# Attention outputs of the last two blocks computed in pairs of tiles on the upper and lower rows of the PE array

## The chip, the cores and the metric

The kernel runs on one core of a Trainium2 chip. The metric is the device time of one execution in microseconds (us); the median of several runs is compared. The core's engines are named as in the profile: PE (TensorE, matrix products; PEld are its weight loads), DVE (VectorE), ACT (ScalarE), POOL (GpSimd) and SP (SyncE, which issues DMAs here).

## The reference

Two kinds of layer alternate, four layers in all, on 2048 tokens of 576 features in bfloat16. Layers 0 and 2 are linear attention with 32 heads of 18 features, layers 1 and 3 an MLP with 4608 hidden units:

```python
x = x + attention(layernorm(x), wqkv, wo)
x = x + mlp(layernorm(x), w1, b1, w2, b2)
x = x + attention(layernorm(x), wqkv, wo)
x = x + mlp(layernorm(x), w1, b1, w2, b2)

# attention, per head
pq, pk = phi(q), phi(k)                  # phi(t) = t + 1 for t > 0, exp(t) otherwise, plus 1e-6
kv, z = pk.T @ v, pk.sum(over tokens)
o = (pq @ kv) / (pq @ z + 1e-6)
out = concat(o over heads) @ wo

# mlp (its input is normalised once more)
h = gelu(layernorm(y) @ w1 + b1)
out = h @ w2 + b2
```

## The kernel before

The tokens are cut into 16 tiles of 128 rows and four blocks of four tiles (c = 0 to 3 in the code; the title's blocks 3 and 4 are c = 2 and 3). A matmul takes a stationary operand, loaded by a weight load of its own, and streams the moving one; the sum over the contracted rows builds up in a bank of PSUM. Everything on PE goes through `mm` (L223, shown as L224 in the profile), which writes PE's order down by hand, in the order of the calls; an `InOrder` wrapper (L45, shown as L53) does the same for DVE, ACT, POOL and SP. So the order of each engine's work is the order of the code.

**Attention outputs.** The 32 heads form five groups, four of seven heads (126 features) and one of four (72, of which 64 rows stand in its own array and the other eight in the spare rows 126 and 127 of the first four groups). `pq[(g, c)]` holds group g of block c, features by tokens; two blocks share one array for group 4, even blocks in rows 0 to 63, odd ones in rows 64 to 127. `kvwo[g]` is the product of kv and wo, 576 columns; for group 4 there are two copies, one with content in the upper 64 rows and zeros below, and `wo_odd` the other way round (L644 to L648). `wo_stage(t)` (L701) makes a tile's output: for each of two halves of 288 columns five matmuls over 128 rows, one for each group, into one bank of a pair of banks; `residual` (L461) then adds both halves to `x_sb` with one DVE instruction.

Ahead of the outputs of a block stands `scales(c)`: DVE multiplies its five `pq` arrays by the reciprocal denominators, which SP's DMAs have spread over the rows (`spread`, L677).

**MLP groups.** `m1_group` (L822) makes four hidden tiles (f = 4g to 4g + 3) for 512 tokens. Here the contraction of 576 is cut at 64 rows: nine products of 64 rows for each tile, 36 in all, issued by turns to the upper and lower 64 rows of the array, which work side by side. Upper rows take the tiles in the order 0, 1, 2, 3, lower rows in the order 2, 3, 0, 1. Two halves of the array never write the same bank at once: before a half goes on with a tile that the other half began, it waits for a relay, a tiny ACT copy (`relay_sb`), which itself waits for the other half's last matmul on that bank (L847 to L867). After that ACT evicts the four tiles through the gelu.

Nine such groups belong to the MLP's first block. Eight of them are already issued within the attention layer, between the output stages, so that PE has work while the denominators go round:

```python
scales(1)
groups(3)
den_stage(2)
den_stage(3)
spread(2)
spread(3)
outputs(1)
scales(2)
scales(3)
groups(3)
outputs(2)
outputs(3)
groups(2)
```

PSUM: `pair` (L73) hands out two double banks by turns, `one` (L85) four single banks by turns. A group takes a pair and two singles, a `wo_stage` a pair.

Of the kernel before, what the change touches and what calls it, by code (L numbers as in the profile page):

```python
# [8 lines left out]
ALU = mybir.AluOpType  # L9
BF16 = mybir.dt.bfloat16  # L10
F32 = mybir.dt.float32
PSUM = bass.MemoryType.PSUM
# [3 lines left out]
P = 128  # L16
# [11 lines left out]
TPC = CB // P  # L28
CA = 512
NCA = S // CA  # L30
HALF = D // 2
# [4 lines left out]
def build(tc, A_x, A_wqkv, A_wo, B_w1, B_b1, B_w2, B_b2, out, n_layers=4):  # L36
    nc = tc.nc
    with ExitStack() as ctx:
        const = ctx.enter_context(tc.tile_pool(name="const", bufs=1))
# [21 lines left out]
        SYNC = mybir.DependencyInfo(mybir.DependencyClass.Sync, mybir.DependencyReason.DATA)  # L61
        vec, act = InOrder(nc.vector, "VectorE"), InOrder(nc.scalar, "ScalarE")
        pool, sp = InOrder(nc.gpsimd, "GpSimd"), InOrder(nc.sync, "SyncE")
# [9 lines left out]
        def pair(name, tag=None):  # L73
            if tag is None:
                pair_turn["n"] += 1
                tag = ("accA", "accB")[pair_turn["n"] % 2]
            return ps_pair.tile([P, 2, 512], F32, name=name, tag=tag)
# [3 lines left out]
        def one_tag():  # L81
            one_turn["n"] += 1
            return f"one{one_turn['n'] % one_turn['banks']}"

        def one(name, tag=None):  # L85
            return ps_one.tile([P, 512], F32, name=name, tag=tag or one_tag())
# [105 lines left out]
        x_sb = const.tile([P, NT, D], BF16, name="x_sb")  # L192
# [12 lines left out]
        wo_odd = const.tile([P, D], BF16, name="wo_odd")  # L205
        kvwo_rows = dpool.tile([8, D], BF16, name="kvwo_rows")
        relay_sb = const.tile([P, 2], F32, name="relay_sb")
        sums_sb = const.tile([P, 4], F32, name="sums_sb")
        y_rows = [dpool.tile([CB, D], BF16, name=f"y_rows{c}") for c in range(NCB)]
        rden_rows = [dpool.tile([H, CA], BF16, name=f"rden_rows{c}") for c in range(NCA)]  # L210
# [6 lines left out]
        def pe(inst):  # L217
            if pe_last["last"] is not None:
                tc.add_manual_dep(inst.ins, pe_last["last"], NOSYNC, reason="TensorE order")
            pe_last["last"] = inst.ins.name  # L220
            return inst

        def mm(out_, lhsT, rhs, start, stop, **kw):  # L223
            return pe(nc.tensor.matmul(out_, lhsT=lhsT, rhs=rhs, start=start, stop=stop, **kw))  # L224


        def load_x(t, by=sp):
# [189 lines left out]
        def by_token(ap, placed):  # L417

            return ap.rearrange("p (t b q) -> p b t q", t=4, b=4) if placed else ap

        def as_read(ap, placed):
            return ap.rearrange("p (b t q) -> p b t q", b=4, t=4) if placed else ap
# [24 lines left out]
        def two(ap):  # L447
            return ap.rearrange("p (h n) -> p h n", h=2)
# [12 lines left out]
        def residual(li, t, halves):  # L461
            xo = xo_of.pop(t)[:] if t in xo_of else x_sb[:, t, :]
            vec.tensor_tensor(out=two(x_sb[:, t, :]), in0=halves, in1=two(xo), op=ALU.add)
            if li == n_layers - 1:
                sp.dma_start(out=out_f[t * P:(t + 1) * P, :], in_=x_sb[:, t, :])

        def layer_A(li, next_kind, begin, before_tile, before_keys, mid_tile, rows_ahead, after_tile, q_tiles, placed, mlp):
            es, pks, kps, vas, pq, ys = {}, {}, {}, {}, {}, {}
            acc = {}
# [23 lines left out]
            def k_finish(t):  # L493
                k_sum(t, 0)
                return k_sum(t, 1)
# [74 lines left out]
            for t in range(NT):  # L570
                before_tile(t)
                if placed:
# [10 lines left out]
                    done = k_finish(t)  # L583
                    if TPC <= t < TPC + NT - NX:
                        ys[t - TPC + NX] = placed_rows(t - TPC + NX)
                else:
# [14 lines left out]
                    if t == 1:  # L601
                        done = k_sum(2, 1)
                    mid_tile(t)
                    rows_ahead(t)
                    if 1 < t < NT - 1:
                        done = k_finish(t + 1)
# [23 lines left out]
            kvwo = {}  # L630
# [70 lines left out]
            def wo_stage(t):  # L701
                c, j = divmod(t, TPC)
                wp = pair("wo_ps")
                for half in range(2):
                    for g in range(G):
# [2 lines left out]
                           by[:, half * HALF:(half + 1) * HALF], g == 0, g == G - 1)  # L708
                residual(li, t, wp[:, :, 0:HALF])


            first = [Norm(t, "B", "act" if t < 3 else "dve", "act" if t == 0 else "dve") for t in range(TPC)]

# [3 lines left out]
                              in1=side[0:126, 0:260].rearrange("p (g c) -> p g c", g=4)[:, :, 64:65].to_broadcast([126, 4, H]),  # L717
                              op=ALU.mult)
            vec.tensor_copy(out=products[0:65, 4, 0:V4].rearrange("p (g d) -> p g d", g=4), in_=tp[0:65, :, 0:126])
            vec.tensor_copy(out=zk[96:P, :].rearrange("p (i c) -> p i c", i=2),  # L720
                            in_=side[96:P, 264:328].unsqueeze(1).to_broadcast([32, 2, 64]))
# [3 lines left out]
                                     in1=sums_sb[96:P, :], op0=ALU.mult, op1=ALU.add)  # L725
            vec.tensor_tensor(
                out=kvT[0:72, 4, 0:72].rearrange("p (h e) -> p h e", h=4),
                in0=side[0:72, 264:336].rearrange("p (h e) -> p h e", h=4),
                in1=maskz[0:72, 0:4, :], op=ALU.mult)
# [3 lines left out]
            for k in range(KD):  # L733
                rows = slice(0, P if k < 4 else 65)
                for g in range(4):
# [5 lines left out]
                              in1=zp[:, 0:1].unsqueeze(1).to_broadcast([P, 2, H]), op=ALU.mult)  # L741
            vec.tensor_tensor(
                out=kvT[0:126, 0:4, :].rearrange("p g (h e) -> p g h e", h=7),
                in0=kvp[0:126, 0:V4].rearrange("p (g h e) -> p g h e", g=4, h=7),
                in1=maskz[0:126, :, :].unsqueeze(1).to_broadcast([126, 4, 7, DH]), op=ALU.mult)
# [40 lines left out]
            def scales(c):  # L786
                for g in range(G):
                    scale_stage(g, c)

            def groups(n):  # L790
                for _ in range(n):
                    mlp.m1_group(0, mlp.done)
                    mlp.flush()

            def outputs(c):
                for t in range(c * TPC, (c + 1) * TPC):
                    wo_stage(t)
# [8 lines left out]
            outputs(1)  # L806
            scales(2)
            scales(3)
            groups(3)
            outputs(2)  # L810
            outputs(3)
            groups(2)

        GF = 4
        NGRP = NF // GF

        class LayerB:
# [4 lines left out]
            def m1_group(self, c, g):  # L822
                hT = self.hT.setdefault(c, {})
                ctok = slice(c * CB, (c + 1) * CB)

                early = [one("h_ps") for _ in range(2)]
                late = pair("hp_ps")
                dst = [late[:, 0, :], early[0][:], late[:, 1, :], early[1][:]]

                def half_blocks(n, hi):  # L830
                    f = g * GF + n
                    rows = slice(64 * hi, 64 * hi + 64)
                    ops = [(n, w1_sb[rows, k, f * P:(f + 1) * P], yT[rows, k, ctok]) for k in range(KD - 1)]
                    if f % 2 == hi:
                        fc = f // 2 * P
                        ops.append((n, w1_tail[rows, fc:fc + P], yT[rows, KD - 1, ctok]))
                    return ops

                upper = [op for n in (0, 1, 2, 3) for op in half_blocks(n, 0)]
                lower = [op for n in (2, 3, 0, 1) for op in half_blocks(n, 1)]  # L840
                seen = [0] * GF
                order = [(hi, n, wt, mv) for step in zip(upper, lower) for hi, (n, wt, mv) in enumerate(step)]
                first, final = {}, {}
                for i, (hi, n, _, _) in enumerate(order):
                    first.setdefault((hi, n), i)
                    final[(hi, n)] = i
                relay_at = {final[(0, 0)]: (0, 2), final[(1, 3)]: (1, 3)}  # L847
                starts = {first[(1, 0)]: 0, first[(0, 2)]: 2, first[(1, 1)]: 1, first[(0, 3)]: 3}
                relay_of = {}

                def evict(n):
                    f = g * GF + n
                    hT[f] = units[:, f, :]
                    out_ = act.activation(out=by_token(hT[f], c > 0), in_=as_read(dst[n], c > 0),
                                          func=ACT.Gelu_apprx_tanh, bias=b1T[:, f:f + 1], scale=1.0)
                    gate["after"] = out_.ins.name

                for i, (hi, n, wt, mv) in enumerate(order):
                    ins = mm(dst[n], wt, mv, seen[n] == 0, seen[n] == 8)
                    seen[n] += 1  # L860
                    if i in starts:
                        tc.add_manual_dep(ins.ins, relay_of[starts[i]], SYNC, reason="row tiles take turns on a PSUM bank")
                    if i in relay_at:
                        relay = act.copy(out=relay_sb[:, 1:2], in_=relay_sb[:, 0:1])
                        tc.add_manual_dep(relay.ins, ins.ins.name, SYNC, reason="row tiles take turns on a PSUM bank")
                        for m in relay_at[i]:
                            relay_of[m] = relay.ins.name  # L867
                        if i == final[(0, 0)]:
                            self.flush()
                    if n in (0, 2) and seen[0] == seen[2] == 9:  # L870
                        evict(0)
                        evict(2)
                    if n == 1 and seen[1] == 9:
                        evict(1)
                self.held = lambda: evict(3)
                self.done += 1

# [209 lines left out]
```

## Time and profile before

| | |
|---|---|
| median of 3 runs | 751.42 us (751.21 to 751.78) |
| the profiled execution | 751.55 us, span 749.8 us |
| PE busy | 745.2 us, 99% of the span |
| DVE, ACT, POOL busy | 269.1, 298.4, 114.9 us |
| outputs of blocks 3 and 4, first attention layer | from 110.7 us of the span on |
| the same, second attention layer | from 478.3 us on |

The span runs from the first to the last instruction of the program. In a timeline's row the columns are start, duration, engine, line, operation, written tile <- read tiles, shape, count, and in brackets the engine's idle time before it and what ended it; consecutive instructions of one kind are merged, and their durations overlap, since matmuls are pipelined. A row of the stages gives for a window its length, then busy time and number of instructions for PE, PEld, DVE, ACT and POOL, the granted clock of PE, and the DMA share and rate. `hp_ps` and `h_ps` are the banks of an MLP group, `wo_ps` those of the outputs, `m_ps` those of the MLP's second product.

### The profile page before, as it was taken

How to read it: one execution, taken by the hardware profiler on the slowest of the kernel's cores; microseconds unless marked ns; L12 is line 12 of the kernel's file. 1: busy time of each engine (PE TensorE's matmuls, PEld its weight loads, DVE VectorE, ACT ScalarE, POOL GpSimd, SP SyncE). 2: the span in 40 equal slices, each digit the busy share in tenths (PEclk: the TensorE clock that was granted, in tenths of full speed). 3: DMA queues.
4: the chain of work that ended last, by engine and by line, in shares of the span. 5: the costliest groups of instructions: out<-in, count | busy, mean ns of one | idle time of the engine just before them, and what ended most of it. 6: DMA issues, size and time to landing. Idle time of an engine off the chain costs nothing.

```text
span 749.8 us, 15361 instructions
## 1 busy us (share of the span) xinstructions
PE 745.2 (99%) x6437; PEld 468.6 (63%) x6437; DVE 269.1 (36%) x654; ACT 298.4 (40%) x652; POOL 114.9 (15%) x245
## 2 busy tenths in 40 slices
PE   9999999999999999999999999999999999999998
PEld 5666455774576457646766665657646754774476
DVE  8987644334124303401365586432400140100000
ACT  5657743106601740374045474440274047205700
POOL 4541100322011201201200020022200120010010
PEclk9999999999999999999999999999999999999999
DMA  7991120022011202110032001102000200020000
GB/s 200 250 354 52 35 68 2 11 49 45 1 27 41 38 1 44 35 26 1 24 109 63 2 9 59 44 1 51 19 1 1 59 10 1 14 46 10 1 12 21
DMA packets 60381, 34.48 MB, mean 46 GB/s; under 512 B 36728, under 2 KB 60312, under 8 KB 60312
## 3 DMA queue, kind: packets, MB, share of 16 engines
q1 hardware_dynamic: 59560, 33.27, 17.4%
q8 instruction: 50, 0.82, 0.4%
q10 hardware_dynamic: 752, 0.23, 0.1%
q14 instruction: 19, 0.16, 0.1%
HBM read 21.70 MB, written 4.93 MB: 36 GB/s over the span
## 4 chain that ended last, share of the span: by engine, by line
PE 99%; DVE 0%; DMA 0%; issue 0%
PE m_ps L224 38%; PE hp_ps L224 21%; PE h_ps L224 17%; PE k_ps L224 6%; PE wo_ps L224 5%; PE q_ps L224 5%; PE rk_ps L224 4%; PE tp L383 1%; PE side_ps L224 1%; PE den_ps L224 0%; PE kvwo_ps L224 0%; PE kv_ps L224 0%; DMA x_sb<-in_A_x_dram 0%; PE rden_ps L224 0%; DVE ln_st L53 0%; PE side_tp L629 0%
## 5 line engine op out<-in xcount | busy, mean ns | idle before, releaser
L224 PEld LDWEIGHTS <-units 128*128 128x128 bf16 x2688 | 260.2, 98 | 74.5 <-issue 4.6
L224 PE MATMUL m_ps<-w_sb,units 128*128 128x288 bf16 (+2 forms) x2304 | 283.6, 286 | 0.0
L224 PEld LDWEIGHTS <-w_sb 64*128 64x128 bf16 x2304 | 123.9, 94 | 136.8 <-ACT relay_sb L53 4.1
L224 PE MATMUL h_ps<-yT,w_sb 64*128 64x512 bf16 x1152 | 178.0, 376 | 0.0
L224 PE MATMUL hp_ps<-yT,w_sb 64*128 64x512 bf16 x1152 | 148.0, 376 | 0.1
L53 DVE TENSOR_TENSOR x_sb<-m_ps,xo 128x576 bf16<-128x576 f32 (+2 forms) x33 | 24.4, 739 | 324.6 <-PE m_ps L224 324.6
L53 ACT COPY relay_sb<-relay_sb 128x1 f32<-128x1 f32 x144 | 27.7, 192 | 264.2 <-PE hp_ps L224 246.6
L53 ACT ACTIVATE units<-hp_ps,b1T 128x512 bf16<-128x512 f32 x144 | 91.2, 684 | 59.3 <-PE hp_ps L224 58.5
L53 POOL TENSOR_TENSOR xo<-x_sb,b_bc 128x576 f32<-128x576 bf16 x32 | 40.8, 1275 | 407.5 <-DVE x_sb L53 298.6
L53 ACT ACTIVATE units<-h_ps,b1T 128x512 bf16<-128x512 f32 x144 | 96.2, 688 | 0.0
L224 PE MATMUL hp_ps<-yT,w_tail 64*128 64x512 bf16 x144 | 54.1, 376 | 0.0
L224 PE MATMUL h_ps<-yT,w_tail 64*128 64x512 bf16 x144 | 54.1, 376 | 0.0
L224 PE MATMUL k_ps<-wkv_sb,yT 128*128 128x288 bf16 (+1 forms) x320 | 52.8, 302 | 0.0
L53 DVE BATCH_NORM_STATS2 ln_st<-x_sb 128x6 f32<-128x288 bf16 x128 | 51.3, 440 | 1.2 <-DMA x_sb<-in_A_x_dram 0.9
L53 ACT ACTIVATE phi_e<-k_ps 128x288 bf16<-128x288 f32 x64 | 26.4, 414 | 52.1 <-PE k_ps L224 50.7
L53 DVE STREAM_TRANSPOSE shared<-y_ring 128x640 bf16<-128x640 bf16 x40 | 32.9, 826 | 39.6 <-DMA yT<-shared 38.0
L53 ACT ACTIVATE units<-q_ps 128x512 bf16<-128x512 f32 x72 | 38.4, 596 | 21.4 <-PE q_ps L224 21.2
L53 DVE TENSOR_SCALAR y_ring<-x_sb,ln_mv,ln_rstd 128x576 bf16<-128x576 bf16 (+2 forms) x58 | 31.1, 538 | 40.7 <-POOL ln_rstd L53 40.5
L224 PE MATMUL q_ps<-yT,wq_sb 128*128 128x512 bf16 (+1 forms) x200 | 44.5, 380 | 0.0
L224 PE MATMUL wo_ps<-shared,units 128*128 128x288 bf16 x288 | 40.7, 286 | 0.0
L224 PEld LDWEIGHTS <-w_tail 64*128 64x128 bf16 x288 | 27.1, 94 | 17.0
L53 POOL TENSOR_TENSOR ln_rstd<-ln_u,neg_half 128x1 f32<-128x1 f32 x64 | 36.1, 564 | 8.5 <-DVE ln_u L53 3.5
(96 smaller groups left out, 421.1 us busy)
## 6 DMA issues: line engine op xcount, KB each, us to landing
yT<-shared SPq DMA_DIRECT2D x160, 40.0 KB
w_sb<-in_B_w_dram SPq DMA_DIRECT2D x12, 432.0 KB
w_sb<-in_B_w_dram SPq DMA_DIRECT2D x9, 512.0 KB
yT<-rden_rows SPq DMA_DIRECT2D x24, 126.0 KB
y_rows<-y_ring SPq DMA_DIRECT2D x16, 144.0 KB
units<-y_rows SPq DMA_DIRECT2D x16, 144.0 KB
x_sb<-in_A_x_dram SPq DMA_DIRECT2D x15, 144.0 KB
out_dram<-x_sb SPq DMA_DIRECT2D x15, 144.0 KB
```

The costliest lines, as they stand in the source:

```text
L53: inst = issue(*args, **kw)
L224: return pe(nc.tensor.matmul(out_, lhsT=lhsT, rhs=rhs, start=start, stop=stop, **kw))
L383: pe(nc.tensor.transpose(out=tp[:, k - a, :], in_=self.y[:, k * P:(k + 1) * P], identity=ident[:]))
```

## The change

The loop that issues 64-row matmuls by turns with its two relays is taken out of `m1_group` into a function, `row_tiles`; the MLP groups call it with ACT's copy as relay and keep their order. A new `wo_pair(t, u)` uses the same function for the outputs of two tiles, t of block 3 and u = t + 4 of block 4. The four accumulators are t's two halves (in a pair of banks) and u's two halves (in two single banks). Each group's product is cut at row 64; group 4 is issued for its 64 rows with content alone. The relay is a memset on POOL of one value per row (`pool_relay`). DVE adds t's halves with one instruction and u's with two. The order of the stages becomes `groups(4)`, four pairs, `groups(1)`, in place of `groups(3)`, eight single tiles, `groups(2)`.

```diff
+        pool_relay = const.tile([P, 1], F32, name="pool_relay")
...
+        def row_tiles(ops_of, dst, relay, after):
+            order = [(hi, op) for step in zip([op for n in (0, 1, 2, 3) for op in ops_of(n, 0)],
+                                              [op for n in (2, 3, 0, 1) for op in ops_of(n, 1)]) for hi, op in enumerate(step)]
+            first, final, total = {}, {}, [0] * 4
+            for i, (hi, (n, _, _)) in enumerate(order):
+                first.setdefault((hi, n), i)
+                final[(hi, n)] = i
+                total[n] += 1
+            relay_at = {max(final[(0, a)], final[(1, b)]): (a, b) for a, b in ((0, 2), (1, 3))}
+            starts = {first[(1, 0)]: 0, first[(0, 2)]: 2, first[(1, 1)]: 1, first[(0, 3)]: 3}
+            relay_of, seen = {}, [0] * 4
+            for i, (hi, (n, wt, mv)) in enumerate(order):
+                ins = mm(dst[n], wt, mv, seen[n] == 0, seen[n] == total[n] - 1)
+                seen[n] += 1
+                if i in starts:
+                    tc.add_manual_dep(ins.ins, relay_of[starts[i]], SYNC, reason="row tiles take turns on a PSUM bank")
+                if i in relay_at:
+                    passed = relay()
+                    tc.add_manual_dep(passed.ins, ins.ins.name, SYNC, reason="row tiles take turns on a PSUM bank")
+                    for m in relay_at[i]:
+                        relay_of[m] = passed.ins.name
+                after(n, [a == b for a, b in zip(seen, total)], relay_at.get(i))
...
+            def wo_pair(t, u):
+                late, early = pair("wo_ps"), [one("wo_ps") for _ in range(2)]
+
+                def ops_of(n, hi):
+                    (c, j), rows = divmod((t, u)[n // 2], TPC), slice(64 * hi, 64 * hi + 64)
+                    tok, cols = slice(j * P, (j + 1) * P), slice(n % 2 * HALF, (n % 2 + 1) * HALF)
+                    ops = [(n, pq[(g, c)][rows, tok], kvwo[g][rows, cols]) for g in range(4)]
+                    if c % 2 == hi:
+                        ops.append((n, pq[(4, c)][rows, tok], kvwo[4][hi][rows, cols]))
+                    return ops
+
+                row_tiles(ops_of, [late[:, 0, 0:HALF], late[:, 1, 0:HALF]] + [acc[:, 0:HALF] for acc in early],
+                          lambda: pool.memset(pool_relay[:], 0.0), lambda *a: None)
+                residual(li, t, late[:, :, 0:HALF])
+                for half, acc in enumerate(early):
+                    rows = x_sb[:, u, half * HALF:(half + 1) * HALF]
+                    vec.tensor_tensor(out=rows, in0=acc[:, 0:HALF], in1=rows, op=ALU.add)
...
-            groups(3)
-            outputs(2)
-            outputs(3)
-            groups(2)
+            groups(4)
+            for t in range(2 * TPC, 3 * TPC):
+                wo_pair(t, t + TPC)
+            groups(1)
...
-                for i, (hi, n, wt, mv) in enumerate(order):
-                    ins = mm(dst[n], wt, mv, seen[n] == 0, seen[n] == 8)
...
+                row_tiles(half_blocks, dst, lambda: act.copy(out=relay_sb[:, 1:2], in_=relay_sb[:, 0:1]), after)
```

More of the change, by code (lines that the diff above doesn't have):

```diff
@@ L837, in half_blocks @@
                     return ops
[L839 to L849, printed above, removed]
                 def evict(n):
@@ L856, in evict, with after @@
                     gate["after"] = out_.ins.name
-                for i, (hi, n, wt, mv) in enumerate(order):
-                    ins = mm(dst[n], wt, mv, seen[n] == 0, seen[n] == 8)
[L860 to L870, printed above, removed]
+                def after(n, done, turn):
+                    if turn == (0, 2):
+                        self.flush()
+                    if n in (0, 2) and done[0] and done[2]:
                         evict(0)
                         evict(2)
-                    if n == 1 and seen[1] == 9:
+                    if n == 1 and done[1]:
                         evict(1)
+                row_tiles(half_blocks, dst, lambda: act.copy(out=relay_sb[:, 1:2], in_=relay_sb[:, 0:1]), after)
                 self.held = lambda: evict(3)
```

## The prediction

> **What bounds the kernel now.** I read the page's header and chain first, then the timeline of PE around the outputs, then the stages. The page:
>
> ```profile
> span 749.8 us, 15361 instructions
> ...
> PE 745.2 (99%) x6437; PEld 468.6 (63%) x6437; DVE 269.1 (36%) x654; ACT 298.4 (40%) x652; POOL 114.9 (15%) x245
> ...
> PE 99%; DVE 0%; DMA 0%; issue 0%
> ```
>
> TensorE (PE) is busy for 745.2 of 749.8 us, and the chain that ends last is 99% PE. So whatever PE time an edit takes away or adds comes out at the end, unless a wait replaces it. The profiled execution took 751.55 us, 1.75 more than its span, and 0.13 above the median of 751.42.
>
> The timeline of PE around block 3 and 4's outputs in the first attention layer:
>
> ```profile
> 110.41 0.38 PE L224 MATMUL h_ps<-yT,w_tail 64*128 64x512 bf16 x1
> 110.72 5.56 PE L224 MATMUL wo_ps<-shared,units 128*128 128x288 bf16 x44
> 116.12 0.29 PE L224 MATMUL wo_ps<-wo_odd,units 128*128 128x288 bf16 x1
> ...
> 120.41 0.29 PE L224 MATMUL wo_ps<-wo_odd,units 128*128 128x288 bf16 x1
> 120.62 1.04 PE L224 MATMUL hp_ps<-yT,w_sb 64*128 64x512 bf16 x8
> ```
>
> Between the two wo_odd rows lie 35 matmuls (seven half tiles of five): 4.29 us, 0.1226 us each. The recorded 0.29 us overlaps the following ones, so the pitch of starts is the cost. An MLP group for comparison, and five matmuls of 512 columns on the full array:
>
> ```profile
> 102.85:106.74 3.89, 3.89 (x40) 1.71 (x37) 1.76 (x5) 2.70 (x8) 0.00 (x0) 1.00 0.32 104
> ```
> ```profile
> 43.53 1.24 PE L224 MATMUL q_ps<-yT,wq_sb 128*128 128x512 bf16 x5
> ```
>
> One group runs from one hp_ps row at 102.85 to that of the next at 106.74: 18 steps, in each of which the upper and the lower 64 rows work at once, 0.216 us a step. Five full-array matmuls of the same width give (1.24 - 0.38)/4 = 0.215. Two 64-row matmuls side by side thus take the time of one full one, and the group keeps that pace through its two relays.
>
> **The change part by part.**
>
> *Removed.* The last 64-row step before the outputs starts at 110.41 and lasts 0.216, so the outputs occupy PE from 110.62 to 120.62. The windows of both layers:
>
> ```profile
> 110.62:120.62 10.00, 10.00 (x82) 7.75 (x81) 5.73 (x8) 1.76 (x4) 0.00 (x0) 1.00 0.01 2
> ...
> 478.18:488.18 10.00, 10.00 (x82) 7.75 (x81) 5.30 (x7) 1.76 (x4) 0.00 (x0) 1.00 0.01 2
> ```
>
> 10.00 us per layer. Of these 80 x 0.1226 = 9.81 are matmuls; the other 0.19 are two gaps of about 0.095, where PE goes from 64-row to 128-row tiles (110.62 to 110.72) and back (120.53 to 120.62).
>
> *Added.* A tile's outputs are two halves of five products over 128 rows, but the fifth has only 64 rows with content. Cut at row 64, a half is nine 64-row products, and a pair of tiles 36: 18 steps of two, in place of 20 full matmuls. Four pairs are 72 steps. I price a step at the full array's 0.1226, as group and q_ps agree at 512 columns: 72 x 0.1226 = 8.83 us. Both gaps go, because the MLP groups on either side are in 64-row tiles already, and from one group to the next the trace has no gap. Per layer 10.00 - 8.83 = 1.17 us saved, in two layers 2.35 (0.38 of it the gaps).
>
> The step's price is not shown at 288 columns. From below it can hardly be under 0.1226, since each half streams the same 288 columns; from above the far end is the group's own 0.216. I take 0.1226, and look at what could stretch it, the weight loads:
>
> ```profile
> 98.62 0.10 PEld L224 LDWEIGHTS <-units 128*128 128x128 bf16 x1
> 98.74 0.29 PE L224 MATMUL wo_ps<-wo_odd,units 128*128 128x288 bf16 x1
> 98.95 0.33 PEld L224 LDWEIGHTS <-w_sb 64*128 64x128 bf16 x6 [0.24 <-issue]
> 98.95 0.61 PE L224 MATMUL hp_ps<-yT,w_sb 64*128 64x512 bf16 x4
> ```
> ```profile
> L224 PEld LDWEIGHTS <-w_sb 64*128 64x128 bf16 x2304 | 123.9, 94 | 136.8 <-ACT relay_sb L53 4.1 <-issue 2.4
> ```
>
> A 64-row load takes 94 ns, and a step needs two. 2304 of them end to end would be 217 us, but they cover 123.9: the loads of the two halves run together. One load of 94 ns fits in a step of 123; a full 128-row load of 0.10 us hides under every wo matmul now.
>
> Here the Trainium skill speaks against the change: "TensorE: Matmul & The Clock Gate", section "Part 3: Packing small matmuls — row/col tiling", has a weight load overlap a running matmul only if it is for other rows of the array. By that each step would be 0.1226 + 0.094. The trace differs: the full-array load just quoted is for the same rows as the matmul running beside it.
>
> The 32 further PE instructions per pair (72 loads and matmuls for 40) come to 33 a microsecond:
>
> ```profile
> 93.16 0.46 PE L224 MATMUL den_ps<-units,zsel 128*32 128x128 bf16 x20
> 93.45 0.23 PE L224 MATMUL den_ps<-ident,eps_sel 128*32 128x128 bf16 x4
> 93.51 0.45 PE L224 MATMUL den_ps<-units,zsel 128*32 128x128 bf16 x20
> ```
>
> The denominators issue 24 matmuls and 24 loads in 0.35 us, so issuing does not bound it.
>
> *The relays.* Each pair has two, eight a layer, as memsets on POOL. The first follows step 5 (both halves leave their bank) and lets step 11 begin; the second follows step 10 and lets step 15 begin. The waiting instruction is a weight load, and behind it stands all of PE, so a late relay is paid in full. No PE to POOL relay is in the trace; its parts are:
>
> ```profile
> 99.83 0.38 PE L224 MATMUL hp_ps<-yT,w_tail 64*128 64x512 bf16 x1
> ...
> 100.30 0.19 ACT L53 COPY relay_sb<-relay_sb 128x1 f32<-128x1 f32 x1 [5.47 <-PE hp_ps L224]
> ```
> ```profile
> 73.90 0.21 DVE L53 BATCH_NORM_AGGREGATE ln_mv<-ln_st 128x2 f32<-128x12 f32 x1
> ...
> 74.20 0.19 POOL L53 TENSOR_SCALAR ln_u<-ln_mv 128x1 f32<-128x1 f32 x1 [0.52 <-DVE ln_mv L53]
> 74.47 0.55 POOL L53 TENSOR_TENSOR ln_rstd<-ln_u,neg_half 128x1 f32<-128x1 f32 x1
> ```
> ```profile
> 1.34 0.10 POOL L53 MEMSET neg_half<- 128x1 f32 x1
> ```
> ```profile
> 108.37 0.21 ACT L53 COPY relay_sb<-relay_sb 128x1 f32<-128x1 f32 x1
> 108.47 0.38 PE L224 MATMUL h_ps<-yT,w_tail 64*128 64x512 bf16 x1
> 108.62 0.15 PEld L224 LDWEIGHTS <-w_sb 64*128 64x128 bf16 x4 [0.28 <-ACT relay_sb L53]
> 108.68 0.38 PE L224 MATMUL hp_ps<-yT,w_sb 64*128 64x512 bf16 x2
> ```
>
> Matmul's end to ACT's relay 0.09; a producer's end to POOL 0.09 (74.11 to 74.20); memset 0.10; relay's end to the load 0.04; load to matmul 0.06, and there PE loses nothing (108.47 + 0.21 = 108.68). Sum from a matmul's recorded end to the next possible matmul: 0.10 + 0.10 + 0.04 + 0.06 = 0.30 us. First relay: step 5 starts at 0.49, ends at 0.78, plus 0.30 is 1.08; step 11 is due at 1.23: 0.15 to spare. Second: step 10 starts at 1.10, ends at 1.39, plus 0.30 is 1.69; step 15 is due at 1.72: 0.03 to spare. So I price the relays at nothing, with the second one thin. If POOL's op took as long as ACT's relay (0.19 to 0.21), it would be 0.08 late: 8 x 0.08 = 0.6 us. POOL has no other work there: the eight memsets are ahead of the next xo, and POOL's share of both windows above is 0.00.
>
> *Moved.* One MLP group, with its matmuls, two ACT relays and four evictions, goes from behind the outputs to ahead of them; the same instructions, no DMA among them. It gives DVE time, for block 4's rows are scaled late:
>
> ```profile
> 109.17 1.89 DVE L53 TENSOR_TENSOR units<-yT,units 128x512 bf16<-128x512 bf16 x5 [4.24 <-DMA yT<-rden_rows]
> ```
> ```profile
> 111.11 1.27 ACT L53 ACTIVATE units<-h_ps,b1T 128x512 bf16<-128x512 f32 x2
> ```
>
> The first pair, which needs block 4 at once, comes at 110.62 + 3.89 = 114.51, long after DVE is done at 111.06. ACT empties the last group's banks 1.76 us after the group's end (112.38 against 110.62); the second pair, which takes these banks, starts 2.21 us after it. Both waits are covered.
>
> *Evictions.* DVE now has one row of 576 and two of 288 per pair:
>
> ```profile
> 119.50 0.76 DVE L53 TENSOR_TENSOR x_sb<-wo_ps,x_sb 128x576 bf16<-128x576 f32 x1 [0.47 <-PE wo_ps L224]
> ```
>
> A 288 one lies between 0.38 and 0.76, so a pair takes DVE 1.5 to 2.3 us, against 2.21 on PE. The banks alternate, so even 2.3 is covered for four pairs; cost nothing.
>
> **Sum.** 751.55 - 2.35 = 749.2 for the profiled execution; against the median 751.42, that is 749.1.
>
> **The rivals.**
>
> *A, the second relay is late.* It does what it says, but POOL's path is longer than the sum of its parts. For it: 0.03 us is all there is. Against: the load can follow a relay and its matmul follow almost at once (98.95 and 98.95 above). 0.1 late gives 749.1 + 0.8 = 749.9, 0.2 late gives 750.7.
>
> *B, the weight loads set the step (slower).* At 288 columns two loads have 0.123 us instead of 0.216. If the halves' loads went one after the other, 2 x 94 = 188 ns, 144 steps would cost 144 x 0.065 = 9.4 us more: 749.1 + 9.4 = 758.5; by the far end, 0.216, 762.5. It decides from a step of 0.139 (2.35/144 = 0.016 above 0.1226). Against it: four loads, two for each half, take 0.15 us together in the row at 108.62.
>
> A load that had to wait for its own rows' matmul would add its whole 0.094 to each step: 144 x 0.094 = 13.5 us, 762.6. The rows of before, which load and multiply on the same rows at once, leave this 0.01 of B's chance. It is the Trainium skill's rule quoted above.
>
> *C, the gain is not on the end's path.* The next wait, such as DVE's evictions at 2.3 us a pair, swallows it: 751.4 less the gaps' 0.4, 751.0. Against: PE's 99%.
>
> **How the numbers follow.** Forecast 0.73 (748.7 to 749.6, from a lower median by the 0.2 to 0.3 that runs differ, to a relay 0.05 late), A 0.18, B 0.06, C 0.03. A measurement of this kernel tells about 0.2% from no change, 1.5 us; faster is below 749.9. That holds the forecast and about a third of A: 0.79. Same: the rest of A and C, 0.15. Slower: B, 0.06. The range runs from 748.7 to 750.6, through A, and leaves out B and C.
>
> **What would show it.** Right: wo_ps starts in twos at a pitch near 0.123; a pair about 2.21 us, no gap at its borders; the stage near 8.8 us; memsets of 0.10 with no PE gap behind. Wrong: a pitch near 0.19 or 0.216 (B), idle PE at steps 11 or 15 with POOL named as releaser (A), or PE waiting for DVE or ACT at a pair's start (C).

## The result and the profile after

The changed kernel takes 748.85 us (median of 6 runs, 748.84 to 749.21), the one before 751.51 in the same comparison: a ratio of 0.9963, 95% interval 0.995 to 0.9976, so 2.7 us or 0.36% faster. The forecast was 749.1, in a range of 748.7 to 750.6.

The page's header and chain of the changed kernel; `mm` now stands in line 225:

```profile
span 747.1 us, 15647 instructions
...
PE 742.5 (99%) x6565; PEld 466.9 (62%) x6565; DVE 268.7 (36%) x662; ACT 298.0 (40%) x652; POOL 116.1 (16%) x261
...
PE 99%; DVE 0%; DMA 0%; issue 0%
```

PE issues 128 matmuls more and is busy 2.7 us less; the span is 2.7 shorter. Nothing took PE's place as the bound. The outputs of blocks 3 and 4 in the first attention layer, on PE's timeline (start, duration, then what; four pairs, of which the first turns of the first one are shown, and the end):

```profile
114.02 0.38 PE L225 MATMUL h_ps<-yT,w_tail 64*128 64x512 bf16 x1
114.23 0.77 PE L225 MATMUL wo_ps<-shared,units 64*128 64x288 bf16 x9
114.72 0.28 PE L225 MATMUL wo_ps<-wo_odd,units 64*128 64x288 bf16 x1
114.84 0.77 PE L225 MATMUL wo_ps<-shared,units 64*128 64x288 bf16 x9
115.34 0.28 PE L225 MATMUL wo_ps<-wo_odd,units 64*128 64x288 bf16 x1
...
122.07 1.14 PE L225 MATMUL wo_ps<-shared,units 64*128 64x288 bf16 x16
123.05 1.03 PE L225 MATMUL hp_ps<-yT,w_sb 64*128 64x512 bf16 x8
```

Ten matmuls, five steps, start between 114.23 and 114.84: 0.122 a step. The first wo_ps row follows the last h_ps step after its usual 0.21, where 0.31 stood before. From 114.23 to 123.05 the stage takes 8.82 us, 72 steps of 0.1225, and the second layer's takes the same:

```profile
114.23:123.05 8.82, 8.82 (x146) 6.83 (x144) 4.46 (x9) 1.75 (x4) 0.79 (x8) 1.00 0.01 2
480.58:489.40 8.82, 8.82 (x147) 6.83 (x145) 4.46 (x9) 1.75 (x4) 0.79 (x8) 1.00 0.01 2
```

The second relay of the first pair, on all engines:

```profile
115.46 0.65 PE L225 MATMUL wo_ps<-shared,units 64*128 64x288 bf16 x8
115.70 0.10 PEld L225 LDWEIGHTS <-units 64*128 64x128 bf16 x2
115.75 0.10 POOL L53 MEMSET pool_relay<- 128x1 f32 x1 [0.57 <-PE wo_ps L225]
```
```profile
115.90 0.15 PEld L225 LDWEIGHTS <-units 64*128 64x128 bf16 x4
```

The step it waits for ends at 115.34 + 0.28 = 115.62, POOL starts 0.13 later, takes 0.10, and the load begins 0.05 after it. Step 15 is due at 114.23 + 14 x 0.1225 = 115.95 and starts then. That is 0.28 to the load where the prediction had 0.24, and it is still in time.

Where do the 2.7 us of the two profiled spans come from? Two landmarks, the first matmul of the kv product (`kv_ps`) and the first of the MLP's second product (`m_ps`), before, after, and in a repeat of the changed kernel (run e9 below):

```profile
60.19 0.79 PE L224 MATMUL kv_ps<-shared,wkv_sb 128*126 128x126 bf16 x11
...
132.38 0.42 PE L224 MATMUL m_ps<-w_sb,units 128*128 128x288 bf16 x2
```
```profile
59.93 1.08 PE L225 MATMUL kv_ps<-shared,wkv_sb 128*126 128x126 bf16 x16
...
130.92 0.42 PE L225 MATMUL m_ps<-w_sb,units 128*128 128x288 bf16 x2
```
```profile
60.19 0.79 PE L225 MATMUL kv_ps<-shared,wkv_sb 128*126 128x126 bf16 x11
...
131.18 0.42 PE L225 MATMUL m_ps<-w_sb,units 128*128 128x288 bf16 x2
```

Between the landmarks lie 72.19 us before, and 70.99 both after and in the repeat: 1.20 less. In the second attention layer it is 72.24 before (427.70 to 499.94) and 71.02 after (426.24 to 497.26), 1.22 less; 2.4 in both. The other 0.26 stand ahead of the first landmark, where the code is the same. I count them as no part of the change: the repeat starts its kv products at 60.19, as before did.

### The profile page after: what moved, and what is told of

It is laid out like the page before. It is cut to its first block, busy times and chain, and to the rows that moved or that the text cites. A ratio compares the mean times of both kernels' runs of the same rounds, so it can differ in the third digit from the quotient of the medians.

```text
span 747.1 us, 15647 instructions
## 1 busy us (share of the span) xinstructions
PE 742.5 (99%) x6565; PEld 466.9 (62%) x6565; DVE 268.7 (36%) x662; ACT 298.0 (40%) x652; POOL 116.1 (16%) x261
## 4 chain that ended last, share of the span: by engine, by line
PE 99%; DVE 0%; DMA 0%; issue 0%
PE m_ps L225 38%; PE hp_ps L225 21%; PE h_ps L225 17%; PE k_ps L225 6%; PE q_ps L225 5%; PE wo_ps L225 5%; PE rk_ps L225 4%; PE tp L409 1%; PE side_ps L225 1%; PE den_ps L225 0%; PE kvwo_ps L225 0%; PE kv_ps L225 0%; DMA x_sb<-in_A_x_dram 0%; PE rden_ps L225 0%; DVE ln_st L53 0%; PE side_tp L655 0%
## 5 line engine op out<-in xcount | busy, mean ns | idle before, releaser
L225 PEld LDWEIGHTS <-units 128*128 128x128 bf16 (+1 forms) x2816 | 258.4, 97 | 74.2 <-issue 4.2
L225 PE MATMUL wo_ps<-shared,units 64*128 64x288 bf16 (+1 forms) x416 | 39.0, 284 | 0.0
```

## The experiments

All times below are medians; "before" in the comparisons of these runs is 751.45 to 751.58. Every run starts from the changed kernel: e1 to e7 with one edit, e8 with that of e7 and one more, e9 with none. Because the first 60 us differ by some tenths from one execution to the next, the stage's own length is the sharper reading.

**e1_move_only: the order of the stages alone.**

```diff
             groups(4)
-            for t in range(2 * TPC, 3 * TPC):
-                wo_pair(t, t + TPC)
+            outputs(2)
+            outputs(3)
             groups(1)
```

> The order of the stages is the changed one (four MLP groups, outputs of blocks 3 and 4, one group), but the outputs are the eight single tiles of before. Theory (the move of a group is free and brings nothing, all of the gain is in the pairs): the time of before, 751.4 +- 0.3; the outputs take 10.00 us of PE in each layer, two gaps of 0.095 included. Rival (the move itself brings a part, because DVE scales block 4 late): 0.4 us a layer less, 750.6.

Measured 751.63 (ratio to before 1.0, interval 0.9991 to 1.0009). The stage, in a window laid as before's was:

```profile
114.81:124.81 10.00, 10.00 (x83) 7.75 (x82) 5.31 (x7) 1.75 (x4) 0.00 (x0) 1.00 0.00 0
```

10.00 us, gaps included. Moving the group is worth nothing by itself.

**e2_pairs_unmoved: the pairs without the move.**

```diff
-            groups(4)
+            groups(3)
             for t in range(2 * TPC, 3 * TPC):
                 wo_pair(t, t + TPC)
-            groups(1)
+            groups(2)
```

> The pairs, but three groups ahead of them and two behind, as before. The first pair then starts near 110.6 us of the span of before, while DVE ends the five scalings of block 4 at 109.60, 109.94, 110.27, 110.61 and 111.06. Theory (the move is cover that the pairs need: PE waits for block 4): up to 0.44 us a layer more than the change, 749.7. Rival (the lower rows take group g only at 110.62 + g x 0.123, the last at 111.11, so each scaling is done just in time): the change's own 748.9, at most 0.1 a layer more.

Measured 749.13 (0.9967, 0.9954 to 0.9979), the change's time. DVE's scalings of block 4 beside the first pair, and the stage's window:

```profile
108.91 1.89 DVE L53 TENSOR_TENSOR units<-yT,units 128x512 bf16<-128x512 bf16 x5 [3.25 <-DMA yT<-rden_rows]
...
110.62 0.77 PE L225 MATMUL wo_ps<-shared,units 64*128 64x288 bf16 x9
```
```profile
110.62:119.44 8.82, 8.82 (x146) 6.83 (x144) 4.64 (x10) 1.76 (x4) 0.80 (x8) 1.00 0.01 2
```

The pair starts at 110.62, before DVE's last scaling ends at 110.80, and PE still loses nothing: the lower rows take the groups one step after another and reach the last at 111.11. The rival stands for this execution. But the scaled array is the operand that is loaded, and the load for that step begins at 110.99, 0.19 after the scaling's end; and the scalings began 0.26 earlier here than in the profile of before (109.17). With the times of before, the last scaling would have ended at 111.06, just at the step's start, so in the first layer it is in part chance that nothing was lost. In the second layer the cover was not needed: there the last scaling ends at 476.34 and the pair starts at 476.99.

**e3_zero_halves: group 4 issued for both halves.**

```diff
-                    if c % 2 == hi:
-                        ops.append((n, pq[(4, c)][rows, tok], kvwo[4][hi][rows, cols]))
+                    ops.append((n, pq[(4, c)][rows, tok], kvwo[4][c % 2][rows, cols]))
```

> The pairs as changed, but group 4's product is issued for both 64-row halves, the one with zeros as well: 40 half products a pair, 20 steps for 18. Theory (the gain is the zero halves left out, 2 steps of 0.1226 in each of 8 pairs, 1.96 us, and four changes of row split, 0.4 us): 748.9 + 1.96 = 750.8, with the gaps at the stage's borders still gone. Rival (two 64-row matmuls side by side gain by themselves, or the zero halves cost nothing): 748.9 to 749.3.

Measured 751.06 (0.9993, 0.9984 to 1.0002).

```profile
114.20:124.00 9.80, 9.80 (x162) 7.80 (x160) 4.46 (x9) 1.76 (x4) 0.80 (x8) 1.00 0.01 2
```

80 steps, 9.80 us, 0.98 more than the change in each layer: 1.96 of the gain is the zero halves left out, as expected. What is left of it, 10.00 - 9.80 = 0.20 a layer, is the two gaps. Working side by side gains nothing of its own.

**e4_act_relay: ACT's copy as relay.**

```diff
-                          lambda: pool.memset(pool_relay[:], 0.0), lambda *a: None)
+                          lambda: act.copy(out=relay_sb[:, 1:2], in_=relay_sb[:, 0:1]), lambda *a: None)
```

> The relays of the pairs are ACT's copy, as in the MLP groups, in place of POOL's memset. Theory (the second relay has 0.03 to 0.05 us to spare, and ACT is still evicting the last group for 1.76 us after the first pair's start): in the first pair of each layer step 11 is 0.8 us late, in the other six pairs the second relay, 0.1 longer, is 0.05 to 0.08 late; 2 x 0.8 + 0.4 = 2.0, 750.9. Rival (the relays have room enough on any engine): 748.9.

Measured 750.44 (0.9985, 0.9977 to 0.9994), 1.6 over the change's 748.85 and 1.3 over its repeat's 749.14; expected were 2.0. The first pair:

```profile
114.88 1.26 ACT L53 ACTIVATE units<-h_ps,b1T 128x512 bf16<-128x512 f32 x2
...
116.02 0.43 ACT L53 COPY relay_sb<-relay_sb 128x1 f32<-128x1 f32 x2
116.27 0.36 PEld L225 LDWEIGHTS <-units 64*128 64x128 bf16 x8 [0.81 <-ACT relay_sb L53]
116.28 0.54 PE L225 MATMUL wo_ps<-shared,units 64*128 64x288 bf16 x6 [0.50 <-ACT relay_sb L53]
```
```profile
114.39:123.96 9.57, 9.07 (x146) 6.67 (x144) 4.46 (x9) 3.17 (x12) 0.00 (x0) 1.00 0.01 2
```

The copy stands behind ACT's evictions and begins only at 116.02, and step 11, due at 114.39 + 10 x 0.1225 = 115.61, starts at 116.28: 0.67 late. The stage is 0.75 longer; the other three pairs share the remaining 0.08, 0.03 each, where I had expected 0.05 to 0.08. So it is the queue, not the copy's length, that would have hurt on ACT.

**e5_long_relay: POOL's relay 0.10 us longer.**

```diff
-                          lambda: pool.memset(pool_relay[:], 0.0), lambda *a: None)
+                          lambda: pool.memset(zk[:], 0.0), lambda *a: None)
```

> POOL's relay is a memset of 128 bfloat16 values a row (0.20 us in the trace of before) in place of one value (0.10); the array is rewritten before its next use. Theory (the second relay of a pair has 0.03 to 0.05 us to spare): 0.10 longer makes step 15 late by 0.05 to 0.07, 8 x that is 0.4 to 0.6, 749.3 to 749.5, and a gap of that size stands at step 15 of every pair, none at step 11. Rival (more than 0.1 to spare): 748.9 and no gap.

Measured 749.53 (0.9974, 0.9964 to 0.9984). The second relay of the first pair, and the stage:

```profile
115.77 0.20 POOL L53 MEMSET zk<- 128x128 bf16 x1 [0.46 <-PE wo_ps L225]
116.03 0.36 PEld L225 LDWEIGHTS <-units 64*128 64x128 bf16 x8 [0.20 <-POOL zk L53]
```
```profile
114.26:123.37 9.11, 9.11 (x148) 6.60 (x145) 4.46 (x9) 1.75 (x4) 1.65 (x8) 1.00 0.01 2
```

Step 15, due at 114.26 + 14 x 0.1225 = 115.97, waits for the load at 116.03. The stage is 0.29 longer, 0.07 a pair. A relay 0.10 longer costs 0.07, so the second one has about 0.03 to spare, as the prediction worked out.

**e6_quarters: twice the weight loads.**

```diff
-                    ops = [(n, pq[(g, c)][rows, tok], kvwo[g][rows, cols]) for g in range(4)]
+                    ops = [(n, q, pq[(g, c)][rows, tok], kvwo[g][rows, cols.start + q * 144:cols.start + q * 144 + 144]) for g in range(4) for q in range(2)]
```

(group 4's product likewise; the accumulator's columns follow q.)

> Each 64-row product of 288 columns is issued as two of 144, each with a weight load of its own: 36 steps a pair for 18, the loads doubled. Theory (the two halves' loads run beside each other and beside the matmuls at a pace well above one per step): a step is near 0.0625, 36 x 0.0625 = 2.25 a pair for 2.21, 8 x 0.04 = 0.4 more, 749.2. Rival (a load's 94 ns has to be over before the next step on its rows): 36 x 0.096 = 3.46 a pair, 10 us more, 759; if the halves' loads go one after the other, 36 x 0.188 = 6.8 a pair, 785.

Measured 749.36 (0.9973, 0.9963 to 0.9983).

```profile
114.29:123.29 9.00, 9.00 (x292) 9.00 (x289) 4.46 (x9) 1.75 (x4) 0.80 (x8) 1.00 0.02 4
```
```profile
L225 PEld LDWEIGHTS <-units 64*128 64x128 bf16 x576 | 18.1, 94 | 0.5
```

144 steps in 9.00 us: 0.0625 each, with two loads of 94 ns in every one. 576 loads of 94 ns in 18.1 busy us (both layers) means that on average three run at a time. Rival B is out: twice the loads, in steps of half the columns, add 0.18 us to the stage, so at 0.1226 a step the loads do not set the pace.

**e7_block2_rows and e8_block2_banks: block 2's outputs on 64 rows too.**

```diff
-            def wo_pair(t, u):
+            def wo_pair(t, u, full=False):
...
-                    if c % 2 == hi:
-                        ops.append((n, pq[(4, c)][rows, tok], kvwo[4][hi][rows, cols]))
+                    if full or c % 2 == hi:
+                        ops.append((n, pq[(4, c)][rows, tok], kvwo[4][c % 2][rows, cols]))
...
-            outputs(1)
+            for t in (TPC, TPC + 2):
+                wo_pair(t, t + 1, True)
```

> On top of the change, block 2's outputs are made in two pairs of 64-row tiles as well, with group 4's zero halves issued (both tiles have their content in the same rows), so 20 steps for 20 matmuls. Theory (a change of row split costs PE 0.1 us, and the one from 128 rows back to the MLP group's 64 goes in each layer): 0.2 us less, 748.6, the gap ahead of the first hp_ps row gone. Rival (the gap is not of the row split, or comes back as a late relay): 748.9 or more.

Measured 749.38 (0.9972, 0.9961 to 0.9982): no gain over the change. Block 2's stage in the changed kernel, and here:

```profile
93.68:98.68 5.00, 5.00 (x47) 3.83 (x41) 3.82 (x5) 0.87 (x2) 0.00 (x0) 1.00 0.11 30
```
```profile
93.75:98.89 5.14, 5.08 (x88) 4.52 (x82) 3.04 (x5) 0.88 (x2) 0.40 (x4) 1.00 0.13 36
```

By the upper half's starts it is 0.14 longer. The first pair's start:

```profile
93.36 1.26 ACT L53 ACTIVATE units<-h_ps,b1T 128x512 bf16<-128x512 f32 x2
...
93.75 0.10 PEld L225 LDWEIGHTS <-units 64*128 64x128 bf16 x2
93.75 1.00 PE L225 MATMUL wo_ps<-shared,units 64*128 64x288 bf16 x8
94.10 0.48 PEld L225 LDWEIGHTS <-units 64*128 64x128 bf16 x9 [0.26 <-issue]
```

The next loads come 0.35 after the first two, where a step is 0.12. The lower rows' first matmul takes a single bank that ACT is still emptying (93.36 + 0.69 = 94.05). The gap behind the stage did go: its last step and the first hp_ps row are 0.12 apart (98.77 and 98.89), where the changed kernel has 0.22 (98.46 and 98.68). But the lower half comes out of the wait another 0.1 us behind the upper one (the last section shows it), so 0.14 is too low a price. From the kv products to the MLP's second product the layers take 71.22 and 71.25, for 70.99 and 71.03 in the repeat of the change: 0.23 and 0.22 more. In the total a start of the kv products at 60.00, 0.19 earlier than in the repeat, hides part of it.

In e8 the first pair writes the two double banks instead, and the second pair the four single ones:

```diff
-            outputs(1)
+            wo_pair(TPC, TPC + 1, True, "pairs")
+            wo_pair(TPC + 2, TPC + 3, True, "singles")
```

> Block 2's outputs in two pairs of 64-row tiles as in e7_block2_rows (group 4's zero halves issued), but the first pair writes the two double banks and the second the four single ones, so that neither waits for ACT's last two evictions. Theory (in e7 the gap of the row split did go, and a wait of 0.23 us for a bank at the first pair's second matmul took its place): the wait goes, the 40 steps with their start take 4.9 us instead of 5.01, and from the kv products to the MLP's second product a layer takes 70.88 for the change's 70.99; 0.2 us less in all, below what the whole time can tell (748.6 for 748.9). Rival (the gap belongs to something else): 70.99 or more.

```profile
94.06:98.98 4.92, 4.92 (x90) 3.91 (x83) 3.39 (x5) 0.88 (x2) 0.40 (x4) 1.00 0.11 28
```

The wait is gone and the stage takes 4.92 for 5.00: the gap of the row split behind it went. No gap came in ahead of it: from the last den_ps row to the first wo_ps row it is 0.16 (93.90 to 94.06), in the changed kernel 0.17 (93.51 to 93.68). The whole time is 748.84 (0.9965, 0.9953 to 0.9978), against 749.14 of the change in the same comparison; the stages account for 2 x 0.08 of these 0.3, which is below what the total can tell. Between the landmarks it is the shortest of all, 70.90 and 70.95 us in the two layers, but the total does not show such a margin.

**e9_change_again: the changed kernel, repeated.**

> The changed kernel once more, on the chip of e8_block2_banks. Theory (0.27 us of the 2.7 between the profiled spans come from the first 10 us, which differ from one execution to the next, and 2.4 from the outputs): from the kv products to the MLP's second product 70.99 and 71.03 us again, whatever the kv products' start is (59.9 to 60.5); 748.8 to 749.2. Rival (the change itself starts faster): the kv products at 59.93 again, and 748.85.

Measured 749.14 (0.9969, 0.9957 to 0.9981). The landmarks, shown above, are 70.99 apart in the first layer again, while the kv products start at 60.19. Over the eleven profiles of this study that start lies between 59.88 and 60.48, and none of the edits touches what runs up to there. What varies was not settled.

## Why the prediction was right, point by point

- **What bounds.** PE's 99% held; what PE saved came out at the end. C (the gain lost to a next wait) is out: the stages show no time beyond the steps, and DVE's three evictions take 1.49 us a pair, the low end of the forecast's 1.5 to 2.3, against 2.21 on PE.
- **The steps.** Priced at 0.1226, measured at 0.1225; 72 steps 8.83, measured 8.82. e3 shows the cause, the two steps of zero halves in each pair.
- **The gaps.** 0.19 a layer expected; e3 and e8 show them go, 0.20 for the two around blocks 3 and 4, 0.08 for one of block 2's. The sum of 2.35 became 2.4: 10.00 - 8.82 = 1.18 in the stage's window, and 0.02 to 0.04 a layer outside it.
- **The weight loads (B).** The argument from four loads in 0.15 us was sound; e6 went to half the step, and the loads kept up. The Trainium skill's rule that a load overlaps only a matmul on other rows ("TensorE: Matmul & The Clock Gate", "Part 3: Packing small matmuls — row/col tiling") does not hold here: in e6 each step of 0.0625 us needs a load of 94 ns for each half, and both PE and PEld are busy for 9.00 of the stage's 9.00 us, so the loads run beside matmuls on the same rows.
- **The relays (A).** Priced at nothing, with 0.03 to spare on the second; e5 measured 0.03. That the two agree is luck in part, since the parts were off in opposite directions: POOL starts 0.13 after the matmul's end, not 0.10, and the matmul can follow its load sooner than 0.06 (in e4 the load starts at 116.27 and the matmul at 116.28).
- **The move.** Priced at nothing, rightly (e1). The reason given, that the pairs need the cover because they take block 4 at once, was too strong: e2 loses nothing without it, since the lower rows need one scaling per step. In the first layer that was close, and an early start of the scalings helped; whether the cover is worth something in a less lucky execution was not tested.
- **Beyond the sum.** The remaining 0.26 of the measured 2.7 lie in the first 60 us and are variation, not the change: that the median came out at 748.85 rather than at the forecast's 749.1 I take for chance, since the repeat's was 749.14.

## What to carry to other kernels

When PE is the bound, count matmul rows that hold only zeros: cutting a contraction at 64 rows gained just those here, beside the two gaps where PE changed its row split, and nothing by working side by side. A relay between the halves needed an engine with an empty queue more than a fast one (0.67 us late behind ACT's evictions, 0.07 for a relay 0.10 longer). Its spare time is the steps from the matmul that it follows to the one that it lets begin, less that matmul's own duration and the hand-overs; price these from the trace and test the sum with a longer relay. Before a stage is moved to other PSUM banks, look up who empties them last.

## What the runs showed of the hardware that I had not expected

Weight loads of 94 ns keep up with a step of 62.5 ns for both halves of the array (e6). Ahead of that run it was no more than its theory; no earlier trace here shows it.

The two halves keep an offset: after the wait in e7 the lower half's matmuls ran about 0.1 us apart from the upper half's, still so at the next MLP group, where both started in the same hundredth before:

```profile
99.76 0.38 PE L225 MATMUL hp_ps<-yT,w_tail 64*128 64x512 bf16 x1
99.86 0.92 PE L225 MATMUL h_ps<-yT,w_sb 64*128 64x512 bf16 x6
```

By the upper half's starts, blocks 3 and 4 then take 0.06 more than in the changed kernel (8.82):

```profile
114.43:123.31 8.88, 8.88 (x147) 8.38 (x144) 4.46 (x9) 1.76 (x4) 0.79 (x8) 1.00 0.01 3
```

This is no further loss. In e7's first two pairs of blocks 3 and 4 the wo_odd row is the lower half's step 5, and the row behind it begins with the upper half's step 6, 0.12 after its step 5:

```profile
115.03 0.28 PE L225 MATMUL wo_ps<-wo_odd,units 64*128 64x288 bf16 x1
115.05 0.77 PE L225 MATMUL wo_ps<-shared,units 64*128 64x288 bf16 x9
...
117.23 0.28 PE L225 MATMUL wo_ps<-wo_odd,units 64*128 64x288 bf16 x1
117.31 0.77 PE L225 MATMUL wo_ps<-shared,units 64*128 64x288 bf16 x9
```

From the first pair to the second, the lower half needs 2.20 us, its usual pace; the upper half needs 2.26, and its lead shrinks from 0.10 to 0.04. So the half that runs behind sets the time, and the price of e7's wait is the 0.23 a layer between the landmarks. Why the upper half fell back there was not tested; I take it for the second relay, which waits for the lower half's later matmul.
